# A dense piece between the halves of the scores, loads spread out, and reciprocals as exp(-ln(sum)) in a fused top-k attention and feed-forward kernel

## The chip, the cores and the metric

The kernel runs on one core of one Trainium2 chip. The metric is the device time of one execution in microseconds; lower is better. The kernel before has a median of 922.19 us over three runs (918.74, 922.19 and 922.97).

Five engines work side by side, each through its own list of instructions in order: TensorE (PE, matrix products; PEld is its loading of weights), VectorE (DVE), ScalarE (ACT), GpSimd (POOL) and SyncE (SP, which here only issues transfers). They wait for each other through semaphores. ScalarE and GpSimd issue transfers from their own lists too.

## The reference, cut to what matters

```python
batch, n_heads, seq, head_dim = (8, 8, 576, 64)
...
scores = scale * np.matmul(q, k.transpose(0, 1, 3, 2))
kth = np.partition(scores, -top_k, axis=-1)[..., -top_k:-top_k + 1]     # top_k = 32
mask = scores >= kth
scores = np.where(mask, scores, -1000000000.0)
scores = scores - np.max(scores, axis=-1, keepdims=True)
attn = np.exp(scores)
attn = attn / (np.sum(attn, axis=-1, keepdims=True) + 1e-09)
out = np.matmul(attn, v)                       # top-k attention, 64 heads
...
x = out.transpose(0, 2, 1, 3).reshape(4608, 512)
h = np.maximum(x @ w_in, 0.0)                  # w_in 512 x 2048
y = h * h @ w_out                              # w_out 2048 x 512
```

For every row of scores the 32 largest of 576 are kept, their softmax weighs the values, and each token's 512 numbers then go through a two-layer network whose middle is squared after the ReLU.

## The kernel before, in words

**Steps.** Everything is driven by a loop over U = 144 steps (`for u in range(U)`, near the end of the listing). A step is two tiles of 128 rows of scores, 576 columns each; nine tiles make a pair of heads, and there are 32 pairs. All engines' lists are written out by hand: `pin` keeps the order in which the code emits the instructions. Work on one tile is spread over several passes of the loop, so in pass u the code emits parts of steps u - 4 to u + 1:

- `drop(u-1)`: ScalarE negates the row maximum and the 32nd value (`neg`, L384); GpSimd marks what lies under the 32nd value (`gone`, L399). The marks are added to the scores `s`, by GpSimd itself in the first 11 steps (`EARLY`, L401), and by a transfer that accumulates later on (L403).
- `quads_of(u)` and `topk(u)`, VectorE: the columns are first folded into maxima and minima of pairs and quads, then four rounds of MAX8 and MATCH_REPLACE8 (L365, L369) find the 32 largest. `quads_of` (L315, L316) reads the tile `most`.
- `invert(u-4)`, VectorE: the reciprocal of the row sums (`rsum`, L465). The sums come with the products of weights and values in a PSUM tile, `av_ps`.
- `scores(u+1)`: TensorE computes the scores in two halves of 288 columns into the PSUM banks `sc_a` and `sc_b` (L284), and ScalarE copies both into `s` (L289). `sc_a` is free again once VectorE's L307 has read it, `sc_b` once L316 has (L306 leaves an interim result there). GpSimd then adds the halves (`both`, L330).
- `prepare`: part of the preparation of a coming pair of heads, with transposes on TensorE through the two PSUM buffers named `gen`, and copies on ScalarE (qkT, qbd, and casts of values).
- `place(u-4)`, ScalarE: the finished rows, scaled by `rsum`, go into `x_tok` (L481) or `x_rem` (L486).
- `exps(u-2)`, ScalarE (L407), then `turn(u-2)`: a transposing transfer from SyncE's list (`wT`, L416). `fetch` issues loads of later pairs on the same list: up to 10 a step while u < 8, 3 afterwards.
- `pairs_of(u+1)`, VectorE (L306, L307, and L309 in the first steps); `copy_far`, ScalarE (the second half of `most`, L322); `lesser`, GpSimd (L339).
- two calls of `dense`, then `products(u-3)`: TensorE weighs the values with `wT` (L451).
- `load_weights(1)`: one load of w_in or w_out from GpSimd's list (L694), 12 in all, three of them ahead of the loop.

**The feed-forward network** is cut into pieces that fill TensorE's gaps. When all 512 numbers of a chunk of 128 tokens are there, `turn_x` puts the chunk's turning into `moves`: four transposes on TensorE into a `gen` buffer (L520) and a copy by ScalarE (`xT`, L526). Afterwards the chunk's block can start: an up piece is 16 matmuls into a `gen` buffer (L569), and on ScalarE a ReLU (`rl`, L574) and a square (`h`, L580); a down piece is 4 matmuls into `dn_ps` (L612), and after the fourth of them ScalarE copies the result (`wide`, L620) and SyncE stores it. `dense` emits at most one turning and one or two pieces; `piece` alternates between ups and downs; with no piece there, `idle_piece` runs four matmuls on constants (L633). A block may start one step after its chunk was turned (`ripe`), in the last 12 steps (`Z`) at the second `dense` of the same step (`fresh`). There, the turning stands right before and between the exponentials instead.

**Behind the loop** the last two steps are turned by TensorE, and what is left of ups and downs is worked off.

The functions that the change touches, and what calls them:

## Time and profile before

| | |
|---|---|
| runs of the kernel before | 922.19, 922.97, 918.74 us |
| the profiled execution | 920.99 us |
| its span, first to last instruction | 919.1 us |
| VectorE busy | 882.8 us, 96% |
| ScalarE busy | 762.3 us, 83% |
| GpSimd busy | 776.8 us, 85% |
| TensorE busy (matmul, weight loads) | 687.5 us, 441.3 us |
| granted TensorE clock, mean | 0.927 |

Times in the profile are us from the span's start unless marked ns. A line of the timeline gives start, duration, engine, source line, operation, what is written and read, and how many were merged; a bracket gives the idle time ahead of it and what ended it. Durations of neighbours on one engine overlap, since an instruction is only done when its last results are written; the distance from one start to the next is what an instruction costs its engine. A line of the waits reads "engine, line waited for: us in total, times, longest". SPq, ACTq and POOLq are the issuing of transfers from those lists.

### The profile page before, as it was taken

The page shows a single profiled execution, that of the slowest core. Times are in us where ns is not written, and L with a number is a line of the kernel's source. Part 1 is how long each engine was busy: PE and PEld are TensorE (multiplying, and loading weights), DVE is VectorE, ACT ScalarE, POOL GpSimd, SP SyncE. Part 2 cuts the span into 40 slices and gives each one's busy share as a digit, 9 for nine tenths or more (in the row PEclk, how much of TensorE's full clock was granted, in tenths as well). Part 3 has the DMA queues.
Part 4 walks back from the last instruction along what each step waited for, and adds up shares of the span by engine and source line. Part 5 has one row for each costly group of instructions (what it writes and reads, how often), then busy time and mean ns, then how long its engine had stood idle before and what let it go on. Part 6 is the DMA issues. An engine that isn't in the chain of part 4 may idle for free.

```text
span 919.1 us, 21088 instructions
## 1 busy us (share of the span) xinstructions
PE 687.5 (75%) x6268; PEld 441.3 (48%) x6268; DVE 882.8 (96%) x3632; ACT 762.3 (83%) x1755; POOL 776.8 (85%) x804
## 2 busy tenths in 40 slices
PE   6766777777677777777776877777787777878777
PEld 3333354445454444444454545454554444555545
DVE  6997999999999999999999999999999999898995
ACT  4655689888988998988988898988988988897884
POOL 7987988888988889888899888988789898787880
PEclk9998989998999999999999799999979998999899
DMA  8597798999997999889898999989899999676762
GB/s 166 78 146 136 155 179 199 195 183 219 181 197 174 203 197 201 197 180 201 195 198 192 197 191 192 203 189 200 177 187 203 198 206 203 141 163 152 167 129 52
DMA packets 290489, 163.60 MB, mean 178 GB/s; under 512 B 258112, under 2 KB 268608, under 8 KB 290368
## 3 DMA queue, kind: packets, MB, share of 16 engines
q1 hardware_dynamic: 267408, 80.29, 46.5%
q0 software_dynamic: 21616, 81.47, 39.9%
q8 instruction: 52, 0.85, 0.4%
q14 instruction: 69, 0.57, 0.2%
q10 hardware_dynamic: 1344, 0.43, 0.2%
HBM read 37.75 MB, written 9.44 MB: 51 GB/s over the span
## 4 chain that ended last, share of the span: by engine, by line
DVE 67%; issue 12%; PE 9%; ACT 7%; DMA 5%; POOL 0%; SPq 0%; ACTq 0%; POOLq 0%; DVEq 0%
DVE m L365 27%; DVE cat L369 18%; DVE sc_b L306 6%; DVE cat L316 5%; DVE cat L315 5%; DVE most L307 5%; DMA s<-gone_b 2%; PE sc_b L284 2%; PE gen L569 2%; PE sc_a L284 1%; DMA wT<-w_two_a 1%; PE dn_ps L612 1%; ACT s L289 1%; DVE rsum L465 1%; ACT x_tok L481 1%
## 5 line engine op out<-in xcount | busy, mean ns | idle before, releaser
L365 DVE MAX8 m<-cat 128x8 f32<-128x104 f32 (+3 forms) x1152 | 438.4, 422 | 0.0
L369 DVE MATCH_REPLACE8 cat<-m,cat 128x104 f32<-128x104 f32 (+2 forms) x864 | 262.9, 311 | 0.0
L330 POOL TENSOR_TENSOR cat<-s 128x576 int32<-128x576 int32 (+1 forms) x144 | 237.9, 1652 | 4.6 <-ACT s L289 4.6
L339 POOL TENSOR_TENSOR cat<-cat,most 128x576 int32<-128x576 int32 (+1 forms) x144 | 195.6, 1359 | 19.3 <-ACT most L322 5.4
L284 PE MATMUL sc_b<-qkT 64*128 64x288 f32 x512 | 106.8, 492 | 116.5 <-DVE cat L316 111.9
L569 PEld LDWEIGHTS <-w_in 128*128 128x128 bf16 x2304 | 155.2, 105 | 46.3 <-issue 25.4
L612 PE MATMUL dn_ps<-w_out,h 128*128 128x512 bf16 x560 | 161.8, 421 | 0.0
L569 PE MATMUL gen<-xT,w_in 128*128 128x128 bf16 x2000 | 144.9, 231 | 7.7 <-ACT xT L526 4.8
L289 ACT ACTIVATE s<-sc_b 128x576 f32<-128x576 f32 x144 | 93.3, 648 | 60.2 <-PE sc_b L284 53.7
L399 POOL TENSOR_SCALAR gone_b<-s,neg 128x576 uint8<-128x576 f32 x142 | 105.9, 746 | 30.9 <-ACT neg L384 21.3
L284 PEld LDWEIGHTS sc_b<-qkT 64*128 64x128 f32 x512 | 46.0, 202 | 167.6 <-issue 87.8
L284 PE MATMUL sc_a<-qkT 64*128 64x288 f32 x512 | 101.0, 470 | 28.3 <-DVE most L307 26.2
L399 POOL TENSOR_SCALAR gone_a<-s,neg 128x576 uint8<-128x576 f32 x143 | 106.6, 745 | 18.1 <-ACT neg L384 7.2
L289 ACT ACTIVATE s<-sc_a 128x576 f32<-128x576 f32 x144 | 91.3, 634 | 23.7 <-PE sc_a L284 21.8
L451 PEld LDWEIGHTS <-wT 128*128 128x128 bf16 (+1 forms) x1600 | 60.1, 103 | 63.9 <-DMA wT<-w_two_c 24.6
L574 ACT ACTIVATE rl<-gen 128x512 f32<-128x512 f32 x141 | 84.3, 598 | 7.1 <-PE gen L569 6.7
L580 ACT ACTIVATE h<-rl 128x512 bf16<-128x512 f32 x136 | 85.7, 630 | 4.3
L612 PEld LDWEIGHTS <-h 128*128 128x128 bf16 x560 | 53.5, 105 | 58.9 <-issue 25.5
L403 POOL DMA_DIRECT2D s<-gone_b x66 | 58.4, 884 | 21.7 <-DVE cat L369 8.1
L403 POOL DMA_DIRECT2D s<-gone_a x65 | 57.4, 883 | 20.2 <-DVE cat L369 10.6
L407 ACT ACTIVATE w_two_a<-s,neg 128x576 bf16<-128x576 f32 x96 | 69.7, 781 | 3.9 <-DMA s<-gone_b 3.4
L407 ACT ACTIVATE w_two_c<-s,neg 128x576 bf16<-128x576 f32 x94 | 68.1, 781 | 3.3 <-DMA s<-gone_b 2.7
(170 smaller groups left out, 1194.8 us busy)
## 6 DMA issues: line engine op xcount, KB each, us to landing
s<-gone_b POOLq DMA_DIRECT2D x66, 576.0 KB, 4.7
s<-gone_a POOLq DMA_DIRECT2D x65, 576.0 KB, 4.7
v_raw<-in_v_dram SPq DMA_DIRECT2D x64, 128.0 KB, 3.2
k_raw<-in_k_dram SPq DMA_DIRECT2D x63, 128.0 KB, 3.6
q_raw<-in_q_dram SPq DMA_DIRECT2D x63, 128.0 KB, 3.2
out_dram<-wide SPq DMA_DIRECT2D x31, 256.0 KB, 3.2
v_raw<-in_v_dram SPq DMA_DIRECT2D x64, 32.0 KB, 3.2
w_in<-in_moe_w_in_dram POOLq DMA_DIRECT2D x8, 256.0 KB, 5.5
```

What stands on the lines that cost most here:

```text
L284: pin(nc.tensor.matmul(out=ps[j][:, x, 0:HALF], lhsT=lhsT, rhs=rhs, start=True, stop=True))
L289: pin(nc.scalar.activation(s[:, :, j * HALF:(j + 1) * HALF], ps[j][:, :, 0:HALF], AF.Copy))
L330: pin(tt(less, s[:, :, 0:wide].bitcast(i32), s[:, :, HALF:HALF + wide].bitcast(i32), op=ALU.add))
L339: pin(tt(less, less, d["most"][:, 0:n_h, :, :].bitcast(i32).rearrange("p h x n -> p x h n"), op=ALU.subtract))
L365: pin(nc.vector.max(out=m[r][:, x, :], in_=part(r, x)))
L369: pin(nc.vector.match_replace(out=part(r, x), in_to_replace=m[r][:, x, :], in_values=part(r, x), imm_value=NEG))
L399: pin(nc.gpsimd.tensor_scalar(byte[:, x, :, 1], s[:, x, :], scalar1=d["neg"][:, x, 1:2], scalar2=-HUGE, op0=ALU.add, op1=ALU.mult))
L403: pin(nc.gpsimd.dma_start(out=s[:, :, :].rearrange("p x n -> p (x n)"), in_=byte[:, :, :, :].rearrange("p x n two -> p (x n two)").bitcast ...
L407: pin(nc.scalar.activation(w_two[u % 3][:, x, 0:S], d["s"][:, x, :], AF.Exp, bias=d["neg"][:, x, 0:1]))
L569: pin(nc.tensor.matmul(out=hp[:, n * n_rows:(n + 1) * n_rows], lhsT=w_in[:, kh, (f0 + n) * 128:(f0 + n + 1) * 128], rhs=xt(kh), start=(kh ...
L580: pin(nc.scalar.activation(h2, flat, AF.Square))
L612: pin(nc.tensor.matmul(out=op[:, :], lhsT=held["h2"][:, f, c * 128:(c + 1) * 128], rhs=w_out[:, f, :], start=(f == 0), stop=(f == NF - 1)))
```

## The change

Line numbers in the profiles of the kernel before are those of the old file. The change does six things.

1. **Reciprocals.** For all steps but the last 12, `invert` is a logarithm of the two sums on ScalarE, and `place` begins with exp(-ln) on ScalarE, which gives `rsum`. A table set that holds both functions is loaded as ScalarE's first instruction; it was loaded ahead of the first copy (L199), behind three load issues.
2. **A dense piece between the halves.** `scores(u+1)` emits the first half, its copy, then `dense(u, 0)` (a turning if there is one, and a piece), and only then the second half and its copy. The second `dense` stays where both were. The order of pieces is fixed: ups first between the halves, downs first in the second call.
3. **A chunk's turning** is queued right after `place` in every step and is emitted between the halves in the next pass; the special places in the last 12 steps go. The block starts at the second `dense` of the pass that turned it.
4. **Loads spread.** `fetch` takes 4 loads a step while u < 12 instead of 10 while u < 8; w_out is loaded in 8 parts instead of 4, so `load_weights` goes on for four more steps.
5. **In the last 20 steps** a step has three pieces: two stood in the first call of `dense` and one in the second; now it is one and two (three in step U - 2).
6. A down block that ended in the second call keeps the next one from starting in the same step.

```diff
+    nc.scalar.preload_act_table_set("natural_log_exp_and_others")
...
-    def scores(u):
+    def scores(u, between=None):
...
+        half(js[0])
+        if not between:
+            half(js[1])
...
             pin(nc.scalar.activation(s[:, :, j * HALF:(j + 1) * HALF], ps[j][:, :, 0:HALF], AF.Copy))
             if u == 0 and j == 1:
                 pairs_of(0)
+            if between and j == js[0]:
+                between()
+                half(js[1])
...
     def invert(u):
-        r = small.tile([128, 2, 1], f32, name="rsum", bufs=4)
-        pin(nc.vector.reciprocal(r[:, :, :], sums(u)[:, :, 64:65]))
-        st[u]["r"] = r
+        r = st[u]["r"] = small.tile([128, 2, 1], f32, name="rsum", bufs=4)
+        if u >= U - 12:
+            pin(nc.vector.reciprocal(r[:, :, :], sums(u)[:, :, 64:65]))
+            return
+        ln = st[u]["ln"] = small.tile([128, 2, 1], f32, name="lnsum", bufs=4)
+        pin(nc.scalar.activation(ln[:, :, :], sums(u)[:, :, 64:65], AF.Ln))
...
     def place(u):
+        if "ln" in st[u]:
+            pin(nc.scalar.activation(st[u]["r"][:, :, :], st[u]["ln"][:, :, :], AF.Exp, scale=-1.0))
...
-                elif at_step[0] >= Z:
+                else:
                     fresh.append(done)
-                else:
-                    ripe.setdefault(at_step[0] + 1, []).append(done)
...
-    def piece(later=False, most=10 ** 6):
+    def piece(later=False, most=10 ** 6, first=None):
         turn_of[0] ^= 1
-        for q_ in ((ups, downs), (downs, ups))[turn_of[0]]:
+        for q_ in ((ups, downs), (downs, ups))[turn_of[0] if first is None else first]:
...
-                if q_ is downs and q_[0].part == 3:
+                if q_ is downs and q_[0].part == 3 and first is not None and phase[0]:
                     shut[0] = at_step[0]
...
     def dense(u, x, later=False):
-        for go in ripe.pop(u, ()):
-            go()
+        phase[0] = x
         if x == 0:
+            ups_now[0] = 0
             if moves:
                 moves.pop(0)()()
-            ups_now[0] = 0
         else:
-            moves.extend(soon_moves)
-            soon_moves.clear()
             while fresh:
                 fresh.pop(0)()
-        N = 2 if u >= U - 20 and x == 0 else 1
-        for n in range(N):
-            if not piece(later, most_ups(u)) and n == 0:
+        for n in range(1 if u < U - 20 or x == 0 else 3 if u == U - 2 else 2):
+            if not piece(later, most_ups(u), (x + n) % 2) and n == 0 and shut[0] != u:
                 idle_piece()
...
-    for g in range(4):
-        rows = moe_w_out.rearrange("(f p) n -> p f n", p=128)[:, 4 * g:4 * g + 4, :]
-        w_loads.append((w_out[:, 4 * g:4 * g + 4, :], rows))
+    for g in range(8):
+        rows = moe_w_out.rearrange("(f p) n -> p f n", p=128)[:, 2 * g:2 * g + 2, :]
+        w_loads.append((w_out[:, 2 * g:2 * g + 2, :], rows))
...
-            scores(u + 1)
+            scores(u + 1, (lambda: dense(u, 0)) if u else None)
...
-        copies = []
-        if u >= Z:
-            turn_x(u)
-            moves.extend(soon_moves)
-            soon_moves.clear()
-            copies = [go() for go in moves]
-            moves.clear()
+        turn_x(u)
+        moves.extend(soon_moves)
+        soon_moves.clear()
         if u == U - 1:
-            copies.pop(0)()
+            moves.pop(0)()()
         if ok(u - 2):
             exps(u - 2, 0)
-            while copies:
-                copies.pop(0)()
             exps(u - 2, 1)
             turn(u - 2)
-        fetch(10 if u < 8 else 3)
+        fetch(4 if u < 12 else 3)
...
         if u < U - 1:
-            dense(u, 0)
+            if u == 0:
+                dense(u, 0)
             dense(u, 1)
...
         products(u - 3)
-        turn_x(u)
         load_weights(1)
```

More of the change, by code (lines that the diff above doesn't have):

```diff
@@ L269, with half @@
     st = {}
-    def scores(u):
+    def scores(u, between=None):
         ps = [ps_sc.tile([128, 2, 512], f32, name=f"sc_{j}") for j in "ab"]
         js = (1, 0) if u < 2 else (0, 1)
-        for j in js:
+        def half(j):
             for x, (i, c, a) in enumerate(steps[u]):
@@ L494 @@
     soon_moves = []
-    ripe = {}
     late, tail = [], []
@@ L636 @@
     behind, fresh = [], []
-    shut = [-1]
+    shut, phase = [-1], [0]
     ups_now = [0]
-    def piece(later=False, most=10 ** 6):
+    def piece(later=False, most=10 ** 6, first=None):
         turn_of[0] ^= 1
-        for q_ in ((ups, downs), (downs, ups))[turn_of[0]]:
+        for q_ in ((ups, downs), (downs, ups))[turn_of[0] if first is None else first]:
             if q_ is ups and ups_now[0] >= most:
@@ L733 @@
     soon.pop(0)()
-    Z = U - 12
     at_step = [0]
@@ L811 @@
             early_exps(u, 1)
-            piece(True)
-            piece(True)
+            piece(True, first=1)
+            piece(True, first=0)
         products(u - 3)
-        turn_x(u)
         load_weights(1)
@@ L825, in flush @@
             behind.pop(0)()
-    assert not ripe and not moves and not soon_moves
+    assert not fresh and not moves and not soon_moves
     late.append(True)
@@ L867 @@
             pin(nc.scalar.activation(bad[:, :], count[0:1, 0:1], AF.Copy))
-    assert not ripe and not moves and not soon_moves
+    assert not fresh and not moves and not soon_moves
     fast.close()
```

## The prediction, made before the changed kernel ran

> **What bounds the kernel now.** I read the page's busy shares first, then its chain that ended last, then VectorE's waits by stretch of time.
>
> ```profile
> span 919.1 us, 21088 instructions
> PE 687.5 (75%) x6268; PEld 441.3 (48%) x6268; DVE 882.8 (96%) x3632; ACT 762.3 (83%) x1755; POOL 776.8 (85%) x804
> DVE 67%; issue 12%; PE 9%; ACT 7%; DMA 5%; POOL 0%; SPq 0%; ACTq 0%; POOLq 0%; DVEq 0%
> ```
>
> VectorE is busy 96% of the span and holds 67% of the chain; everyone else has air. Its idle time sits in few places. The answers below are its waits in 50 to 92 us (steps 7 to 11), 92 to 780 and 780 to 880; each row gives who waited for whom, the us in total, the times and the longest.
>
> ```profile
> DVE rsum L465 <- PE av_ps L451: 4.8, 3, 2.7
> DVE sc_b L306 <- ACT s L289: 1.0, 3, 0.3
> DVE cat L315 <- ACT most L322: 0.9, 1, 0.9
> ...
> DVE cat L315 <- ACT most L322: 1.6, 4, 0.9
> DVE rsum L465 <- PE av_ps L451: 1.0, 1, 1.0
> ...
> DVE rsum L465 <- PE av_ps L451: 5.3, 3, 2.6
> DVE sc_b L306 <- ACT s L289: 1.1, 1, 1.1
> DVE cat L315 <- ACT most L322: 0.4, 1, 0.4
> ```
>
> So 6.7 us are lost early, 2.6 us in the 688 us of the middle, 6.8 us late. One step of the middle on VectorE:
>
> ```profile
> 510.73 0.16 DVE L465 RECIPROCAL rsum<-av_ps 128x2 f32<-128x2 f32 x1
> 510.81 0.45 DVE L365 MAX8 m<-cat 128x8 f32<-128x120 f32 x2
> 513.14 0.45 DVE L306 TENSOR_TENSOR sc_b<-sc_a,s 128x288 f32<-128x288 f32 x1
> 513.87 1.41 DVE L365 MAX8 m<-cat 128x8 f32<-128x576 f32 x2
> 519.14 0.45 DVE L306 TENSOR_TENSOR sc_b<-sc_a,s 128x288 f32<-128x288 f32 x1
> 521.20 0.43 DVE L315 TENSOR_TENSOR cat<-sc_b,most 128x288 f32<-128x288 f32 x1
> ```
>
> A step is 519.14 - 513.14 = 6.00 us, VectorE's own work without a gap. What the others do in a step counts only once it no longer fits.
>
> **Reciprocals (L465): -10.6 us.** A reciprocal lasts 0.16 us, but its successor starts after 510.81 - 510.73 = 0.08 us: consecutive instructions overlap. 132 of 144 go to ScalarE, so 132 x 0.08 = 10.6 us, and a step becomes 5.92 us. Taking 0.16 each would promise 21 us, which the overlap denies. The 4.8 + 1.0 + 5.3 = 11.1 us that the reciprocals waited do not go by themselves: on TensorE the late products (L451) stand ahead of the next scores, so VectorE would wait at L306 instead. For the same reason the new wait on ScalarE, Ln for those products, costs nothing of its own, though the s copies, the squares and the exponentials are queued behind it: the first s copy needs scores that TensorE issues after the products.
>
> **Loads spread (SyncE's queue, steps 0 to 11): -3.2 us of the early 6.7.** SyncE's queue, ScalarE and TensorE around the first early wait:
>
> ```profile
> 43.83 1.34 SPq L110 DMA_DIRECT2D q_raw<-in_q_dram  x2
> 49.84 1.28 SPq L117 DMA_DIRECT2D v_raw<-in_v_dram  x2
> 51.23 2.00 SPq L416 DMA_TRANSPOSE wT<-w_two_a  x1
> ...
> 46.02 1.44 ACT L407 ACTIVATE w_two_a<-s,neg 128x576 bf16<-128x576 f32 x2
> ...
> 57.34 0.54 PEld L451 LDWEIGHTS <-wT 128*128 128x128 bf16 x10 [5.53 <-DMA wT<-w_two_a]
> ```
>
> The weights were ready at 46.02 + 1.44 = 47.46, but ten loads held the queue from 43.83 to 51.12, so the transpose went out 3.8 us late and TensorE waited 5.5 us for it. In the changed order 4 loads (6 once) stand between two transposes, 2.9 us at this rate; that wait goes. What is late next is GpSimd, whose queue also issues the weight loads:
>
> ```profile
> 36.99 0.74 POOL L399 TENSOR_SCALAR gone_b<-s,neg 128x576 uint8<-128x576 f32 x1
> 42.88 0.56 POOL L694 DMA_DIRECT2D w_in<-in_moe_w_in_dram  x1
> 43.52 0.74 POOL L399 TENSOR_SCALAR gone_a<-s,neg 128x576 uint8<-128x576 f32 x1
> ...
> 89.01 0.75 POOL L399 TENSOR_SCALAR gone_a<-s,neg 128x576 uint8<-128x576 f32 x1
> 96.25 1.57 POOL L399 TENSOR_SCALAR gone_b<-s,neg 128x576 uint8<-128x576 f32 x2
> ...
> 93.55 0.21 ACT L384 ACTIVATE neg<-m 128x4 f32<-128x4 f32 x1 [1.15 <-DVE m L365]
> ```
>
> Its round with a weight load is 43.52 - 36.99 = 6.53 us, of which the load takes 43.52 - 42.88 = 0.64. The round that ends at 96.25 has no load and takes 7.24 us, since it still does the last early masking and already the wide sums; at its end GpSimd is 96.25 - 93.55 = 2.7 us behind the value it needs, and VectorE does not feel that. After the change the loads go on to step 12 (8 halves of w_out, as large as a w_in load, in place of 4), and VectorE no longer pauses so that GpSimd can catch up. Estimate: rounds 2 to 9 lose 0.3 us each against VectorE's early step, rounds 10 and 11 lose 7.24 + 0.64 - 6.0 = 1.9 each: 8 x 0.3 + 2 x 1.9 = 6.2 us behind, where 2.7 was harmless. So 3.5 of the 6.7 us come back as waits for GpSimd's results. Bounds: nothing gained, and all 6.7.
>
> **Table load first (L49 of the changed kernel): +1.3 us.**
>
> ```profile
> 0.76 0.67 ACTq L142 DMA_DIRECT2D k_raw<-in_k_dram  x1
> 2.82 1.28 ACT L199 ACT_TABLE_LOAD   x1 [2.82 <-issue]
> 4.14 1.09 PE L188 MATMUL gen<-id_f,k_raw 128*128 128x128 f32 x4 [4.14 <-DMA k_raw<-in_k_dram]
> ```
>
> Now it lies behind ScalarE's three load issues, hidden by the flight of the loads; then it stands ahead of them, and TensorE's first work waits for k. Its 1.28 us are the most that it can cost; nothing, if an issue can pass a running table load. I take 1.3, as the row shows the two one after the other.
>
> **A dense piece between the halves, and ln/exp on ScalarE: +4 us in the middle.** TensorE and ScalarE in the middle:
>
> ```profile
> 512.19 1.06 PE L569 MATMUL gen<-xT,w_in 128*128 128x128 bf16 x16
> 516.15 0.76 PE L284 MATMUL sc_b<-qkT 64*128 64x288 f32 x4 [1.29 <-DVE cat L316]
> ...
> 516.17 0.19 ACT L384 ACTIVATE neg<-m 128x4 f32<-128x4 f32 x1
> 516.27 0.63 ACT L289 ACTIVATE s<-sc_a 128x576 f32<-128x576 f32 x1
> 519.83 0.41 ACT L322 ACTIVATE most<-sc_b 128x288 f32<-128x288 f32 x1
> 520.12 0.61 ACT L574 ACTIVATE rl<-gen 128x512 f32<-128x512 f32 x1
> 520.76 0.63 ACT L580 ACTIVATE h<-rl 128x512 bf16<-128x512 f32 x1
> 521.31 0.21 ACT L384 ACTIVATE neg<-m 128x4 f32<-128x4 f32 x1
> ...
> 120.00:780.00 660.00, 495.43 (x4663) 323.11 (x4662) 657.39 (x2736) 586.53 (x1357) 578.10 (x567) 0.92 0.94 194
> ```
>
> TensorE stands idle 1.29 us before the second half, because that bank is free only after L316; an up piece lasts 1.06 us, so it fits there for nothing. ScalarE pays. The last row (busy PE, PEld, DVE, ACT, POOL of 120 to 780 us, PEclk, DMA share, GB/s) gives it 586.53 of 660 us, 5.33 us a step. The trace has no Ln; the nearest row is neg, as small: 0.10 us to the next start (516.27 - 516.17). The Exp feeds the x_tok copies right behind it, so its whole 0.2 us count and a gap, as rl before h takes 0.64 for 0.61. Together 0.33 us (bounds 0.2, both by starts, and 0.45, both whole), so 5.66 of 5.92 us: 96% full. That fits, but order matters too. L315 waits for the most copy; here that ended at 520.24, 0.96 us ahead of L315 at 521.20. After the change rl, h (0.64 + 0.55), Ln and Exp stand ahead of it: 1.5 us more. Against that, neg may start sooner: its MAX8 ended at 513.87 + 1.41 = 515.28, and it ran at 516.17 because rl and h came first; 0.9 us back. Net 0.6 us later: some 0.35 us of slack are left, and none in a step that also copies one of the 32 turned chunks (rl's size). I charge such a step 0.1 us, and a little for stretches of slow clock: 4 us in all. Bounds: 0, and 36 (0.3 us in 120 steps, if neg gains nothing).
>
> A rule bears on the clock; PEclk is 0.92 in that row. The Trainium skill (TensorE: Matmul & The Clock Gate, "Part 1: The HAM clock gate (the "warmup" mystery)") says that TensorE's clock is halved after a window of about 3.4 us with too little activity. By it, a piece moved into the gap would raise PEclk, and the 4 us would be nearer 2.
>
> **Late stage: -1.5 us.** The copy of a turned chunk now follows the first s copy, so the next piece gets its PSUM buffer sooner; but steps 124 to 130 hold two pieces and ln/exp. Of 6.8 us I take 1.5 back (bounds: 6 back, 3 more lost). What is left to do behind the last step is the same work.
>
> **Sum** on the profiled execution's 920.99 us (1.89 beside its span): -10.6 - 3.2 + 1.3 + 4 - 1.5 = -10.0, so 911. That execution stands 1.2 us under the runs' median of 922.19 and within their spread, so I shift nothing.
>
> **Rivals.**
> - ScalarE is full: its addition is nearer 0.45 us, and each middle step loses 0.08 us more: 120 x 0.08 = 9.6, about 921. For it: 96% full. Against: L315's waits in the middle are only 1.6 us now.
> - Slower: most is late in every step, because neg gains nothing from the new order (output copies, value casts and late scores keep ScalarE busy until then). At 0.3 us a step the middle loses 36 instead of 4: 943. It decides against the change from 0.15 us a step (the gain of 10.0, the 4 charged, and 4.6 for half a per cent, over 120 steps). Against: the 0.9 us above.
> - Better: GpSimd's backlog is harmless, the middle has no new stalls, the table load is hidden, 5 of the late waits go: 920.99 - 10.6 - 6.7 - 5 = 899.
> - Not what it says: each Ln and each Exp loads a table, 264 x 1.28 = 338 us, about 1250. Against: in the changed program's order ScalarE has one table load, and Copy, Relu and Exp share one in this trace. The Trainium skill (ScalarE: Activation LUTs, "Table sets: the hidden batching unit") names a set with both exp and ln, which speaks against it too.
>
> **How the numbers follow.** Forecast 911 (902 to 918): 0.50. Better, 899: 0.17. ScalarE full, 921: 0.18. Slower, 943: 0.14. Tables: 0.01. The range 899 to 922 leaves out the slower cases and a little on either side. A measurement of this kernel can tell about 0.5% from no change: under 917.6 is faster (0.66, a little of the forecast's case being above), over 926.8 slower (0.15), the rest 0.19.
>
> **What would show it.** Right: VectorE steps of 5.92 us in the middle; L315 waiting for most there 3 to 6 us; no wait for wT before 80 us, but waits at 80 to 105 us that end at GpSimd or at s; TensorE's first matmul near 5.4 us; ScalarE 95% busy. L315's waits over 18 us are the slower rival. Steps still at 6.00 would make the first term wrong, early waits of under 1 us the second.

## The result, and the profile after

The changed kernel took 929.64 us (median of 6 runs) beside 922.36 us for the kernel before in the same job: ratio **1.0119, 95% interval 1.0082 to 1.0157**. The ratio is formed from fast executions alone (one of the six, 944.18 us, was slow), so it isn't the quotient of the two medians, 1.008. Forecast were 911 us and a faster kernel; it became slower. In the profile of after, the old L306, L315, L322, L451, L465 and L481 are L315, L324, L331, L460, L475 and L495.

From the page of after, span, busy shares and the chain that ended last, by engine and by line:

```profile
span 927.1 us, 21006 instructions
PE 678.1 (73%) x6186; PEld 422.6 (46%) x6264; DVE 878.4 (95%) x3500; ACT 792.7 (86%) x2019; POOL 780.0 (84%) x808
...
DVE 34%; ACT 22%; DMA 13%; PE 9%; issue 8%; SPq 1%; POOL 1%; ACTq 0%; POOLq 0%; DVEq 0%
DVE m L374 13%; DVE cat L378 9%; ACT s L295 4%; DMA wT<-w_two_b 4%; DMA wT<-w_two_a 4%; PE gen L580 3%; DMA wT<-w_two_c 3%; DVE sc_b L315 3%; ACT rl L585 3%; ACT h L591 3%; DVE cat L324 3%; DVE most L316 3%; DVE cat L325 2%; ACT w_two_c L416 2%; PE sc_a L286 2%
```

VectorE's busy share fell by a point only, but its share of the chain was halved, from 67% to 34%. In its place stand ScalarE (22% for 7%) and transfers (13% for 5%), all of these named being transfers of wT. A chain that was one engine's has become a chain through four. That is the first thing to look at when a kernel whose bound engine was relieved gets no faster.

Where the time went: the three stretches up to step 20, steps 20 to 120, and the rest, cut at the starts of VectorE's first instruction of a step (columns: length; busy time of PE, PEld, DVE, ACT, POOL; PEclk, DMA share, GB/s). Before, then after:

```profile
9.22:140.76 131.54, 94.69 (x646) 53.73 (x646) 123.36 (x505) 85.15 (x202) 112.62 (x123) 0.92 0.81 145
140.76:742.51 601.75, 450.23 (x4226) 291.67 (x4227) 600.32 (x2501) 535.00 (x1238) 527.99 (x516) 0.93 0.94 194
742.51:919.10 176.59, 138.37 (x1384) 93.36 (x1382) 158.42 (x626) 139.58 (x314) 128.24 (x126) 0.93 0.70 149
```

```profile
9.20:136.84 127.64, 92.32 (x637) 48.12 (x646) 122.03 (x490) 88.92 (x234) 115.08 (x126) 0.95 0.82 149
136.84:755.01 618.17, 449.35 (x4185) 286.09 (x4239) 597.93 (x2402) 558.09 (x1438) 528.21 (x517) 0.95 0.91 190
755.01:927.10 172.09, 132.09 (x1350) 85.85 (x1365) 157.75 (x610) 143.09 (x346) 128.79 (x126) 0.97 0.73 152
```

The first stretch gave 131.54 - 127.64 = 3.9 us, the last 4.5, and the hundred steps between took 618.17 - 601.75 = 16.4 us: together +8.0, which is 927.1 - 919.1. The middle is the whole question. VectorE's waits there (112 to 780 us), and ahead of them those of 80 to 112 us:

```profile
DVE cat L324 <- ACT most L331: 2.5, 2, 1.9
DVE m L374 <- POOL cat L348: 2.0, 2, 1.5
...
DVE sc_b L315 <- ACT s L295: 9.8, 9, 3.6
DVE cat L324 <- ACT most L331: 9.5, 20, 0.9
```

All of the middle's waits end at ScalarE. One place shows how. Four steps of after, one window each, and three of before:

```profile
526.88:532.82 5.94, 4.45 (x58) 2.67 (x58) 5.94 (x26) 5.33 (x14) 5.34 (x7) 1.00 0.98 224
532.82:538.75 5.93, 5.00 (x37) 3.50 (x35) 5.93 (x26) 4.81 (x12) 5.38 (x7) 0.71 0.74 161
538.75:545.41 6.66, 5.24 (x47) 3.02 (x46) 6.03 (x26) 6.56 (x19) 4.69 (x5) 1.00 0.76 170
545.41:551.47 6.06, 3.80 (x39) 2.54 (x40) 6.04 (x25) 5.92 (x18) 5.24 (x6) 1.00 0.95 223
```

```profile
519.14:525.14 6.00, 4.09 (x23) 1.72 (x22) 6.00 (x26) 4.51 (x12) 5.45 (x7) 0.71 1.13 228
525.14:531.14 6.00, 6.00 (x63) 4.67 (x62) 6.00 (x26) 5.11 (x13) 4.97 (x6) 0.72 0.79 178
531.14:537.14 6.00, 4.81 (x58) 3.38 (x54) 6.00 (x26) 5.97 (x15) 5.10 (x7) 1.00 1.06 172
```

The first two rows show the step that was forecast: 5.93 to 5.94 us for 6.00 before. In the second, PEclk is 0.71, because TensorE's clock was halved for 3.41 us. ScalarE fell behind in it: its exponentials began 0.75 us ahead of this step (532.07) and 1.00 us behind the start of the next (539.75). The next step held 6.56 us of work for it, VectorE waited, and the step took 6.66. Before, two steps in a row at 0.71 and 0.72 cost nothing. The trace's records of the granted clock have 22 such stretches in steps 20 to 120 of before (88.7 us, and 1.8 us lost over 100 x 6.00), and 17 in after (61.4 us, and 25.2 lost over 100 x 5.93). Of after's loss 20 us lie in the 34 steps in or just behind a stretch. So it isn't the clock that got worse; the slack that absorbed such stretches is gone. That the stretches cause the loss isn't shown by this: a step that stalls also gives TensorE less to do.

What has no slack is a circle that takes two steps. In steps 20 to 120 the chain that ended last passes through a transfer of wT fifteen times in after (91 us), and never in before. One such turn, from the timeline of after (rows of TensorE, ScalarE and SyncE's queue that make the circle; a bracket is the idle time and what ended it):

```profile
575.87 1.43 ACT L416 ACTIVATE w_two_b<-s,neg 128x576 bf16<-128x576 f32 x2
577.33 2.32 SPq L425 DMA_TRANSPOSE wT<-w_two_b  x1
...
584.12 0.48 PE L460 MATMUL av_ps<-vau_a,wT 128*128 128x65 bf16 x10 [3.25 <-DMA wT<-w_two_b]
584.53 0.76 PE L286 MATMUL sc_a<-qkT 64*128 64x288 f32 x4
585.22 1.07 PE L580 MATMUL gen<-xT,w_in 128*128 128x128 bf16 x16
...
586.33 0.60 ACT L585 ACTIVATE rl<-gen 128x512 f32<-128x512 f32 x1 [0.26 <-PE gen L580]
586.96 0.63 ACT L591 ACTIVATE h<-rl 128x512 bf16<-128x512 f32 x1
587.49 0.63 ACT L295 ACTIVATE s<-sc_b 128x576 f32<-128x576 f32 x1
588.02 0.59 ACT L176 ACTIVATE qkT<-gen 128x512 f32<-128x512 f32 x1
588.50 0.20 ACT L487 ACTIVATE rsum<-lnsum 128x2 f32<-128x2 f32 x1
588.73 0.52 ACT L495 ACTIVATE x_tok<-av_ps,rsum 128x64 bf16<-128x64 f32 x2
589.14 1.44 ACT L416 ACTIVATE w_two_a<-s,neg 128x576 bf16<-128x576 f32 x2
```

The exponentials (575.87) are turned by a transfer (577.33), for which the products wait until 584.12; behind them in TensorE's list stand the first scores and the piece between; behind that piece, in ScalarE's list, rl, h, the second copy of s, a copy that prepares a coming pair (qkT), Exp, x_tok, and the exponentials of two steps later (589.14). That is 589.14 - 575.87 = 13.27 us where two steps are 11.86. Behind them the copy of most came late, and VectorE waited 0.60 us for it at 590.91.

Half clock can't be the only trigger, since the granted clock was 1.00 throughout this turn. Fourteen of the fifteen turns lie wholly in these steps, from 12.0 to 16.8 us long; in six of them the clock was full, and these took 12.0 to 13.3. Long transfers may be another: the fourteen took 4.9 to 7.4 us from issue to landing (6.75 here), where the medians of all transfers, by the three buffers that they read, are 4.1 to 4.6. In before these medians are 4.9 to 5.2, and little was lost: there, rl and h belonged to pieces behind the top-k work and ran behind the copy of most, so the second copy of s waited for no piece of its own step.

### The profile page after: what moved, and what is told of

It is laid out like the page before. It is cut to its first block, busy times and chain, and to the rows that moved or that the text cites. A ratio compares the mean times of both kernels' runs of the same rounds, so it can differ in the third digit from the quotient of the medians.

```text
span 927.1 us, 21006 instructions
## 1 busy us (share of the span) xinstructions
PE 678.1 (73%) x6186; PEld 422.6 (46%) x6264; DVE 878.4 (95%) x3500; ACT 792.7 (86%) x2019; POOL 780.0 (84%) x808
## 4 chain that ended last, share of the span: by engine, by line
DVE 34%; ACT 22%; DMA 13%; PE 9%; issue 8%; SPq 1%; POOL 1%; ACTq 0%; POOLq 0%; DVEq 0%
DVE m L374 13%; DVE cat L378 9%; ACT s L295 4%; DMA wT<-w_two_b 4%; DMA wT<-w_two_a 4%; PE gen L580 3%; DMA wT<-w_two_c 3%; DVE sc_b L315 3%; ACT rl L585 3%; ACT h L591 3%; DVE cat L324 3%; DVE most L316 3%; DVE cat L325 2%; ACT w_two_c L416 2%; PE sc_a L286 2%
## 5 line engine op out<-in xcount | busy, mean ns | idle before, releaser
L374 DVE MAX8 m<-cat 128x8 f32<-128x104 f32 (+3 forms) x1152 | 439.7, 423 | 2.0 <-POOL cat L348 2.0
L339 POOL TENSOR_TENSOR cat<-s 128x576 int32<-128x576 int32 (+1 forms) x144 | 235.1, 1633 | 10.6 <-ACT s L295 8.1
L348 POOL TENSOR_TENSOR cat<-cat,most 128x576 int32<-128x576 int32 (+1 forms) x144 | 195.9, 1361 | 41.6 <-ACT most L331 32.0
L580 PEld LDWEIGHTS <-w_in 128*128 128x128 bf16 x2304 | 145.2, 103 | 41.8 <-issue 37.5
L460 PEld LDWEIGHTS <-wT 128*128 128x128 bf16 (+1 forms) x1600 | 60.0, 100 | 211.6 <-issue 56.4
L623 PE MATMUL dn_ps<-w_out,h 128*128 128x512 bf16 x490 | 131.3, 384 | 7.8 <-issue 4.4
L408 POOL TENSOR_SCALAR gone_a<-s,neg 128x576 uint8<-128x576 f32 x143 | 106.6, 745 | 14.3 <-ACT neg L393 1.7
L315 DVE TENSOR_TENSOR sc_b<-sc_a,s 128x288 f32<-128x288 f32 x144 | 65.7, 456 | 14.8 <-ACT s L295 12.1
L324 DVE TENSOR_TENSOR cat<-sc_b,most 128x288 f32<-128x288 f32 x144 | 63.9, 444 | 15.5 <-ACT most L331 13.9
L623 PEld LDWEIGHTS <-h 128*128 128x128 bf16 x560 | 50.0, 99 | 58.0 <-issue 19.6
L412 POOL DMA_DIRECT2D s<-gone_a x65 | 57.4, 884 | 20.2 <-DVE m L374 12.8
```

The source lines that it names most:

```text
L339: pin(tt(less, s[:, :, 0:wide].bitcast(i32), s[:, :, HALF:HALF + wide].bitcast(i32), op=ALU.add))
L348: pin(tt(less, less, d["most"][:, 0:n_h, :, :].bitcast(i32).rearrange("p h x n -> p x h n"), op=ALU.subtract))
L374: pin(nc.vector.max(out=m[r][:, x, :], in_=part(r, x)))
L408: pin(nc.gpsimd.tensor_scalar(byte[:, x, :, 1], s[:, x, :], scalar1=d["neg"][:, x, 1:2], scalar2=-HUGE, op0=ALU.add, op1=ALU.mult))
L412: pin(nc.gpsimd.dma_start(out=s[:, :, :].rearrange("p x n -> p (x n)"), in_=byte[:, :, :, :].rearrange("p x n two -> p (x n two)").bitcast ...
L580: pin(nc.tensor.matmul(out=hp[:, n * n_rows:(n + 1) * n_rows], lhsT=w_in[:, kh, (f0 + n) * 128:(f0 + n + 1) * 128], rhs=xt(kh), start=(kh ...
```

## The experiments

Three theories stood at the start. **LOOP**: the circle just shown. **RING**: a shorter one of one step, through the products' single bank `av_ps` (x_tok, products, sc_a, piece between, rl, h, s, Exp, x_tok). **FULL**: ScalarE has too little slack, whatever the order. Ratios are to the kernel before, in the same job; "lost" is the length of steps 20 to 120 less 100 unstalled steps (593 us with logarithms, 600 with VectorE's reciprocals), in one profiled execution. It is good to some 7 us: before, e7 and e8 have the same steps there and lost 1.8, 1.9 and 8.6 (4.9 of the last in one wait), and e1 and e13, alike there too, 3.4 and 6.8.

### First job: parts of the change

**e1, no piece between the halves** (the turning too goes back to the step's end):

```diff
-            scores(u + 1, (lambda: dense(u, 0)) if u else None)
+            scores(u + 1)
...
-            if u == 0:
-                dense(u, 0)
+            dense(u, 0)
             dense(u, 1)
...
         products(u - 3)
+        if u < U - 2:
+            turn_x(u)
```

> The changed kernel (929.6 us; VectorE's steps 20 to 120 take 618.2 us there, 601.8 before) with both dense calls back behind the top-k, all else kept: ln/exp on ScalarE, loads spread. Theory RING: the dense piece between the halves closes a ring that has to go round once a step: x_tok copies (ScalarE) free the only bank of av_ps, products (TensorE), first half of the scores, up piece, rl and h (ScalarE), second copy of s, Exp, x_tok. Without the piece the ring is some 2 us shorter: steps 20 to 120 in 593 to 598 us, total 904 to 910 us. Theory FULL: ScalarE simply has too much to do since ln and exp came to it; the place of the piece does not matter: steps 20 to 120 stay near 618, total near 927 to 930.

926.27 us, 1.0065 [1.0033, 1.0097]; the profiled execution is its fastest (919.82). There the middle was 596.4 us, 3.4 lost, but steps 120 to 143 took 148.9 us for 141.9 in after. The piece between costs the middle and pays late; neither theory had the late loss.

**e2, all reciprocals on VectorE**, the rest as in after:

```diff
-        if u >= U - 12:
+        if True:
```

> The changed kernel with all reciprocals on VectorE again, the piece still between the halves. FULL: ScalarE is relieved by 0.33 us a step, so the waits go and VectorE's step is 6.00: steps 20 to 120 in 601 to 604 us, total 911 to 915 us. RING: the ring is only 0.3 us shorter against a step that is 0.08 us longer, so many of the waits stay: steps 20 to 120 in 608 to 615, total 918 to 926.

919.98 us, 0.9989 [0.9954, 1.0024]. Its profiled execution was its slowest (928.0 us, 14.9 lost), so here the runs decide: without the logarithms the kernel is as fast as before. That lies in RING's range (918 to 926), not in FULL's (911 to 915).

**e3, the piece's ScalarE part late** (rl, h and wide of the piece between behind the copy of most; the matmuls stay):

```diff
-            scores(u + 1, (lambda: dense(u, 0)) if u else None)
+            scores(u + 1, (lambda: dense(u, 0, True)) if u else None)
...
+            while behind:
+                behind.pop(0)()
```

> The changed kernel; TensorE's part of the piece stays between the halves, but ScalarE's part of it (rl and h, or wide) is emitted behind the most copy as in the kernel before. ScalarE's work is the same in sum. RING: rl and h are out of the ring (1.2 us, and the wait for the up piece), steps 20 to 120 in 593 to 600 us, total 904 to 911. FULL: nothing changes, 927 to 930.

943.15 us, 1.0255 [1.0193, 1.0317]. The middle was as long as in after (618.2 us, 25.2 lost), and its 12 us more came behind step 120 (939.2 - 756.0 = 183.2 us for 172.1). Neither theory had expected that. The trace shows why the middle gained nothing: the second copy of s still stands behind the piece, since TensorE does the second half of the scores after it. Waits of ScalarE for that half in 112 to 780 us of after, then of this kernel:

```profile
ACT s L295 <- PE sc_b L286: 2.6, 6, 0.8
```

```profile
ACT s L295 <- PE sc_b L286: 39.8, 44, 2.3
```

In after the second copy of s began 0.28 us (median) behind the end of those scores, here 0.05. So taking rl and h out shortened the circle by 0.2 to 0.3 us only, not by their 1.2, and the chain passes through transfers of wT sixteen times, as often as in after. Why the end of the kernel was slower stays unexplained.

**e4, logarithms alone**, put into the kernel before with the early table load (items as in the change):

```diff
+        ln = st[u]["ln"] = small.tile([128, 2, 1], f32, name="lnsum", bufs=4)
+        pin(nc.scalar.activation(ln[:, :, :], sums(u)[:, :, 64:65], AF.Ln))
```

> The kernel before with ln/exp on ScalarE and the table load first, nothing else of the change. RING: the step becomes 5.93 and the waits stay away, steps 20 to 120 in 594 to 598 us; the early waits stay, moved from the reciprocal to L306; total 909 to 914 us. FULL: ScalarE's waits come here as well, steps 20 to 120 in 610 to 618, total 922 to 930.

922.98 us, 1.0008 [0.9975, 1.0041], with unstalled steps of 5.93 us that should have been worth 1.1%. In its profile, of its slowest execution (926.11 us), 11.7 were lost in the middle, and VectorE waited 10.4 us for ScalarE (112 to 780 us). The saving of VectorE isn't seen in the runs, even with no piece between.

### Second job: the circles, and the loads

**e5, x_tok first**: Exp and the x_tok copies ahead of the copies of the scores.

```diff
+            if ok(u - 4):
+                place(u - 4)
             scores(u + 1, (lambda: dense(u, 0)) if u else None)
```

> The kernel after, with one step moved: the Exp of the sums' logarithms and the copies of the weighted values into x_tok are put into ScalarE's order ahead of the copies of the scores of the next step, instead of behind both of them and the chunk work between. Theory RING (products, av bank, x_tok and the piece between the halves hang on each other once per step): x_tok no longer waits for sc_a, the up piece, rl, h and s_b, the wait of TensorE's first product (L460) for x_tok goes from 64 us to under 10, and steps 20 to 120 fall from 618 us to 593 to 600; total 904 to 914. Theory LOOP (the exponentials, the wT transfer, the products and the chunk work between take two steps together, and nothing is over): the loop still holds s_b ahead of the exponentials, so the middle stays at 612 to 620 and the total at 925 to 932. Theory FULL (ScalarE has too little slack): the same work, 925 to 932.

933.97 us, 1.0119 [1.0042, 1.0196], 24.1 lost. The wait for x_tok vanished from TensorE's list of waits, the waits for wT stayed (122 us, of TensorE's weight loads in 112 to 780 us), and so did the loss. RING falls.

**e6, products a step later**, up to the 112th step, with a fourth buffer of wT and a seventh of the values:

```diff
+        w = u - 5 if u <= C + 1 else u - 4
...
-        products(u - 3)
+        if u <= C:
+            products(u - 4)
```

> The kernel after, with products, sums and placing of x one step later in all steps up to the 112th (one more buffer of wT and one more of the values), so that a block has three steps instead of two from its exponentials to its products. Nothing else is moved and no work is added. Theory LOOP (two steps through the wT transfer are full): TensorE's and its weight load's waits for wT (83 us and 152 us after) go to under 20 each, steps 20 to 112 run at 5.93 to 5.98 each, and the total is 904 to 912. Theory RING (the av bank's one step): its order is unchanged, so the middle stays at 612 to 620 and the total at 925 to 932. Theory FULL: 925 to 932.

919.47 us, 0.9976 [0.9940, 1.0013]; the middle fell from 618.2 to 607.3. Waits for wT and x_tok in 112 to 780 us of after, then of this kernel:

```profile
PE av_ps L460 <- ACT x_tok L495: 55.3, 57, 1.6
PEld L460 <- DMA wT<-w_two_a: 48.6, 32, 3.0
PEld L460 <- DMA wT<-w_two_b: 48.3, 30, 4.2
...
PEld L460 <- DMA wT<-w_two_c: 38.8, 31, 4.0
```

```profile
PE av_ps L460 <- ACT x_tok L495: 88.1, 95, 2.7
...
PEld L460 <- DMA wT<-w_two_a: 3.5, 3, 1.8
PEld L460 <- DMA wT<-w_two_c: 3.3, 3, 1.7
PEld L460 <- DMA wT<-w_two_b: 2.4, 3, 1.0
```

135.7 us of the weight loads' waiting for wT became 9.2, the chain passes through a transfer of wT once instead of fifteen times, and the ratio fell by 1.4%. TensorE's longer wait for x_tok did no harm that e10 could find. LOOP is right in kind, and too large in size: it expected 904 to 912.

**e7, loads spread** alone in the kernel before, and **e8**, the same with w_out still in four loads:

```diff
-        fetch(10 if u < 8 else 3)
+        fetch(4 if u < 12 else 3)
```

> The kernel before, with the loads alone spread as in the kernel after (four a step for 12 steps instead of ten for 8; w_out in eight loads of half the size). No theory of the middle touches it: steps 20 to 120 as before, 600 to 603. Steps 0 to 12 fall by 7 to 8 us against before, steps 12 to 16 rise by 4 to 5 where GpSimd catches up (as in the kernel after), and the total is 915 to 919 if these two do not depend on the piece between; if they do, 920 to 925.

> The kernel before, with the loads spread over 12 steps but w_out still in four loads. If the stall in steps 12 to 16 is GpSimd catching up on the work that the faster first steps bring sooner, it stays (28 to 29 us for four steps, against 24 before) and the total is as with the loads spread and w_out halved. If the smaller w_out loads make it, the stall goes and the total is 3 to 5 us lower, 911 to 915.

923.21 us, 1.0022 [0.9985, 1.0059], and 920.24 us, 0.9976 [0.9941, 1.0011]. In their profiles steps 0 to 20 took 128.2 and 129.2 us for 131.5 before; the runs as a whole show no gain that can be told from none. Steps 12 to 20 took 53.2 and 52.9 us for 49.4: the stall there doesn't come from the halved loads.

### Third job: is it the step, and what is left?

**e9**, a fourth buffer of wT and nothing else; then products later with x_tok first (**e10**), with no piece between (**e11**), and with reciprocals by VectorE (**e12**); the edits are those above, put together.

```diff
-name="wT", bufs=3)
+name="wT", bufs=4)
```

> The kernel after with four buffers of wT instead of three, and nothing else. Putting the products a step later brought the ratio from 1.012 to 0.998, and that kernel had four such buffers too. If it was the buffer (the transposing DMA waiting for the products to free one), this one falls as far: 917 to 922, middle (steps 20 to 120) 605 to 610. If it was the third step between exponentials and products (theory LOOP), this one stays at 926 to 933, middle 614 to 620, with wT waits on TensorE of 60 to 90 us.

> The kernel after with the products a step later (steps up to the 112th) and the copies of x_tok ahead of the copies of the scores: both changes that were made singly before. The later products alone left a middle of 607 us over an ideal 593, with 88 us of TensorE's products waiting for x_tok. If the rest is that one-step loop (RING now behind LOOP), the wait goes under 10 us, the middle comes to 593 to 599 and the total to 905 to 914. If ScalarE's lack of slack makes the rest (FULL), the middle stays at 604 to 612 and the total at 915 to 925.

> The kernel after with the products a step later and both chunk pieces behind the top-k work as in the kernel before (no piece between the halves); the reciprocals by ScalarE and the spread loads stay. With the piece behind alone the ratio was 1.0065, with a middle of 597. LOOP and RING both leave nothing here: middle 593 to 596, and the total is what the late steps leave, 910 to 920. If FULL still costs something, the middle is 597 to 605 and the total 918 to 926.

> The kernel after with the products a step later and all reciprocals by VectorE. An unstalled step is then 6.00 us, a middle of 600, instead of 5.93. If ScalarE's 0.25 us a step of Ln and Exp makes what is left over in the later-products kernel (607 against 593), this one's middle is 600 to 603, with waits of VectorE under 3 us, and the total 915 to 922: the gain of the reciprocals is given back in full. If something else makes the rest, it shows here too: middle 607 to 614, total 923 to 930.

The buffer: 929.03 us, 1.0108 [1.0071, 1.0146]. It was the step, not the buffer of wT (the seventh of the values wasn't tried alone). With x_tok first: 922.72 us, 1.0015 [0.9996, 1.0035], 11.4 lost; RING isn't behind LOOP either. With no piece between: 936.41 us, 1.0179 [1.0136, 1.0221], 12.8 lost, and steps 120 to 143 took 153.6 us. That was a miss on both accounts and stays unexplained; its granted clock, 0.909, was among the lowest. With VectorE's reciprocals: 919.64 us, 0.9983 [0.9956, 1.0011], 5.0 lost, as FULL expected. It equals the same kernel with logarithms (0.9976): as far as the runs can tell, ScalarE's share gives the gain back in full.

Steps 20 to 120 of the kernel with logarithms alone, of products later, and of products later with VectorE's reciprocals:

```profile
141.50:746.18 604.68, 446.70 (x4177) 292.67 (x4227) 595.87 (x2401) 557.63 (x1439) 528.01 (x516) 0.92 0.92 193
```

```profile
138.60:745.94 607.34, 441.19 (x4195) 282.29 (x4248) 596.19 (x2401) 558.67 (x1443) 529.36 (x517) 0.97 0.93 193
```

```profile
138.42:743.40 604.98, 440.04 (x4205) 281.11 (x4257) 601.38 (x2503) 534.68 (x1240) 529.82 (x517) 0.97 0.92 194
```

ScalarE (the fourth busy time) has 558 us to do in the first two, 94% of 593 unstalled us, and 535 in the third, 89% of 600. The kernels with 558 lose 11.7 and 14.3 us there, the one with 535 loses 5.0. These are single executions: e8, with 535, lost 8.6, and e1 and e13, with 556 and 557, 3.4 and 6.8. So FULL rests on the ratios of the runs; that the busy time sets the loss isn't shown.

### Fourth and fifth job: the clock, and a better order

**e13, piece between from step 124 on only** (the turning at the step's end up to there), and **e16**, the same with VectorE's reciprocals:

```diff
-            scores(u + 1, (lambda: dense(u, 0)) if u else None)
+            scores(u + 1, (lambda: dense(u, 0)) if u >= U - 20 else None)
```

> The kernel after with the piece and the chunk's turning between the halves of the scores only from step 124 on; up to there both pieces stand behind the top-k work and the turning at the step's end. Theory: the piece between costs in the middle alone, where every step is close to full, and pays in the last twenty steps. Steps 20 to 120 then run as with no piece between (597), steps 124 to 143 and the tail as in the kernel after (118 and 30), and the total is 908 to 916, below both kernels. Rival: the late steps owe their gain to blocks that the piece between finished earlier, and then 124 to 143 stays at 122 to 126 and the total at 918 to 926.

> The kernel of e13 with all reciprocals by VectorE, so that of the change only the spread loads and the order of the last twenty steps are left. If the logarithms gain in the middle what they seem to (7 us less what they lose by waits, some 4 us net where no piece stands between), this one is 3 to 6 us slower than e13: 912 to 920. If ScalarE's extra work loses as much as VectorE gains, it is equal to e13 or faster, 908 to 914.

918.62 us, **0.9960 [0.9938, 0.9982]**, and 920.40 us, 0.9984 [0.9961, 1.0007]. The first is the only kernel whose interval lies under the kernel before. It is 0.4%, not the 1% hoped for, and the two aren't told apart. Its steps 124 to 143 took 120.8 us, between the 118 of the theory and the 122 of its rival. Steps 20 to 120 of the first:

```profile
139.84:739.64 599.80, 452.85 (x4238) 296.65 (x4238) 595.08 (x2401) 556.98 (x1439) 529.01 (x517) 0.92 0.95 195
```

6.8 us are lost, less than half of the loss with the logarithms and the piece between.

**e14, half of each down piece, and e15, half of each up piece**: in the steps up to 124 every second matmul with w_out, or with w_in, is left out.

```diff
-                for f in range(4 * part, 4 * part + 4):
+                fs = range(4 * part, 4 * part + 4)[::2 if at_step[0] < U - 20 else 1]
+                for f in fs:
```

> The kernel after, leaving out half of the products with w_out in the steps up to 124 (two matmuls of 512 columns instead of four per down piece, so its output is not the reference's). The piece between the halves is an up piece in most steps and keeps its whole length; TensorE has some 0.45 us a step less to do behind the top-k work. Theory CLOCK (the loop is just full, and stretches at half clock are what it cannot take): fewer such stretches, under 8 of them in steps 20 to 120 instead of 17, and the middle falls to 596 to 606. Theory LENGTH (the piece between is too long at any clock): the middle stays at 612 to 620.

> The kernel after, leaving out half of the products with w_in in the steps up to 124 (eight matmuls of 128 columns instead of sixteen per up piece, so its output is not the reference's). The piece between lasts about half as long. Theories CLOCK and LENGTH both expect the middle at 594 to 602; if it stays above 608, neither TensorE's length nor its clock is in the loop, and ScalarE's order alone (rl and h ahead of the copies of the scores) is.

Their middles, half down pieces first:

```profile
138.96:768.66 629.70, 449.68 (x4038) 290.72 (x4039) 600.91 (x2401) 560.37 (x1438) 529.12 (x517) 0.87 0.88 186
```

```profile
138.46:753.45 614.99, 441.86 (x3438) 250.51 (x3439) 597.30 (x2402) 559.66 (x1435) 527.80 (x517) 0.88 0.92 191
```

Both expectations were turned round: 940.13 us, 1.0165 [1.0122, 1.0208], and 928.38 us, 1.0066 [1.0039, 1.0093]. TensorE had less to do, its granted clock fell from 0.95 to 0.87 and 0.88, and half-clock time rose from 61 us to 160 and 143. The middle lost 36.7 and 22.0 us. A lighter TensorE got a lower clock. What a stretch costs can't be read from these runs: with half down and half up pieces, 74 and 73 of the hundred steps lie in or behind a stretch, and hold nearly all of the loss (35 and 22 us), but in before 65 do, and hold 1.8.

**e17 and e18, filler**: two matmuls of 382 columns into an unread part of the bank `av_ps`, in after ahead of the products, and in the kernel of e13 between the halves.

```diff
+            pin(nc.tensor.matmul(out=avb[:, 130:512], lhsT=id_h[:, :], rhs=fill[:, 0:382], start=True, stop=True))
```

> The kernel after with two matmuls of 382 columns ahead of the products in the steps up to 124, into a part of the products' bank that nobody reads: TensorE has some 0.4 us a step more to do, at the place where it waits 1.4 us a step for wT and x_tok. Theory CLOCK (half-clock stretches, which come when TensorE has too little to do, are what the full loop cannot take): under 8 half-clock stretches in steps 20 to 120 instead of 17, granted clock 0.98 or more, the middle 600 to 610, total 912 to 922. Rival (the clock goes along, it does not cause): the clock may rise, but the middle stays at 614 to 622, total 926 to 934.

> The kernel of e13 (piece between only from step 124) with the same two filler matmuls between the halves of the scores up to step 124, where TensorE waits 0.7 us a step for sc_b to come free. Theory CLOCK: the half-clock time of steps 20 to 120 falls from 96 us to under 50, the middle from 599.8 to 594 to 597, total 911 to 917. Rival: there is slack enough without a piece between, so that the clock is worth nothing, and the filler's 0.4 us delays sc_b in part of the steps: middle 599 to 606, total 918 to 925.

933.58 us, 1.0138 [1.0107, 1.0168], and 988.45 us, 1.0738 [1.0706, 1.0769]. The second was no test: the filler had to wait for the logarithm that reads the same tile, as TensorE's first wait shows (L646 is the filler there).

```profile
PE av_ps L646 <- ACT lnsum L481: 130.8, 77, 3.1
```

The first raised the granted clock to 0.98 and halved the half-clock time (27 us), and still lost 21.6 us, as the rival expected; but its filler too waited for x_tok (92.5 us), so its 0.4 us lie inside the circle. What the clock alone is worth stays open.

## Why the prediction was wrong, point by point

- **Reciprocals, -10.6.** The size of the unstalled step was right: 5.93 to 5.94 us for a forecast 5.92. That this reaches the end was wrong. Three pairs that differ in the logarithms alone (the first in the early table load too) show it: before and e4 (1.0008), e12 and e6 (0.9983 and 0.9976), e16 and e13 (0.9984 and 0.9960). Of the forecast 1.1%, between -0.1 and 0.24% is left, and each ratio is uncertain by 0.2 to 0.4% either way; and in after itself the logarithms cost 1.3% (e2).
- **Loads spread, -3.2.** Right in the profile, in mechanism and nearly in size: step 20 was reached 3.9 us sooner, after 74.7 us for steps 0 to 12 (82.2 before) and 52.9 for 12 to 20 (49.4). Some 1.1 of that are reciprocals (16 x 0.07); the five profiles with spread loads and VectorE's reciprocals (e2, e7, e8, e12, e16) gained 1.6 to 3.3 there. The waits that came back stand where they were expected, at 92 to 109 us, and begin at GpSimd: 2.0 us straight (`L374 <- POOL cat L348`), and the longest, 1.9 us for most, behind exponentials that waited 2.6 us for the transfer of GpSimd's marks (`s<-gone_a`). In the runs of the loads alone it can't be seen.
- **Table load, +1.3.** Wrong, it cost no more than 0.1. The rows below show ScalarE loading its table and issuing a transfer at the same time; TensorE began at 4.23 us for 4.14 before.

```profile
0.76 1.28 ACT L49 ACT_TABLE_LOAD   x1 [0.76 <-PEq L982]
0.79 0.66 ACTq L143 DMA_DIRECT2D k_raw<-in_k_dram  x1
...
4.23 1.09 PE L189 MATMUL gen<-id_f,k_raw 128*128 128x128 f32 x4 [4.23 <-DMA k_raw<-in_k_dram]
```

- **Piece between and logarithms on ScalarE, +4. This is the step that failed**: it measured 25.2 - 1.8 = 23 us. Two sentences of it are wrong. "An up piece lasts 1.06 us, so it fits there for nothing" counted TensorE's gap, the engines' loads and, for ScalarE, how late the copy of most would be. It didn't follow the piece, rl and h further: ahead of the second copy of s, and through it of the exponentials and the transfer for the products two steps on. That circle was never added up; giving it one more step (e6) took back 11 us of the middle and 1.4% of the time. And "a little for stretches of slow clock" took the slack of before for granted, in which 22 such stretches stood beside a loss of 1.8 us. ScalarE's addition itself was sized somewhat too high: 0.28 us a step by the distances to the next start (medians of 0.05 behind Ln and 0.23 behind Exp), 0.23 by busy time (535.00 / 100 to 558.09 / 100), for a forecast 0.33.
- **The rule on the clock.** PEclk of the middle rose from 0.93 to 0.95, and it fell to 0.87 when down pieces were halved. Both agree with the Trainium skill (TensorE: Matmul & The Clock Gate, "Part 1: The HAM clock gate (the "warmup" mystery)"), by which too little activity halves the clock. That the 4 us would thus be nearer 2 was wrong: the clock rose and the middle lost 23 us more.
- **Late stage, -1.5.** 4.5 us were gained behind step 120 (172.1 us for 176.6), inside its bounds, so the term was too small by 3. The logarithms have no visible part in it: e2 and e12, without them, took 171.6 and 171.8 us there. This is the part of the change that pays, but e13, which keeps only the order of the last twenty steps, took 175.0 us and so holds 1.6 of the 4.5.
- **The rivals.** "ScalarE is full" (921) and "most late in every step" (943) lie on both sides of 929.64. The waits for most came to 9.5 us in 20 places, far from every step; as much again (9.8) was lost earlier in the step, at L315, because the copy of s was late. No rival named the circle.

What the runs show: the loss needs the circle through wT and the logarithms both, since giving the circle a step (e6) or taking the logarithms out (e2) brings the time back to that of before, and doing both (e12) brings no more. The chain agrees: it passes a transfer of wT fifteen and sixteen times in the middles of after and e3, once in those of e6, e1, e10 and e11; between them stand e2's slowest execution (ten) and e4's (six). What stays open: why e3 and e11 lost as much late as they did; why e11's middle, without the circle in its chain, lost 12.8 us; and how much of the loss is triggered by half clock and how much by long transfers.

## What to carry to other kernels

Before moving work between engines, add up the circles, not only the loads: follow each result through every engine's list until it comes back to its own buffer or list, in us, and compare that with the steps it may take. A gap of one engine isn't free if something behind the filler, in another engine's list, feeds the next turn of such a circle. And a saving on the bound engine is worth what the next engine has to spare: with ScalarE at 94% of the step, VectorE's 0.07 us a step brought no gain clear of noise in any of three pairs of kernels.

## What the runs showed of the hardware

- TensorE's granted clock fell when its work was reduced: 0.95, 0.88 and 0.87 with whole pieces, half up and half down pieces, and 0.98 with filler added ahead of the products (e17). Of the 589 half-clock stretches in the twenty traces, 571 last 3.41 us or a multiple of it.
- A table load of 1.28 us ran on ScalarE beside the issuing of transfers from its own list.
- Ln and Exp of 128 x 2 values last 0.15 and 0.20 us and added 0.23 us a step to ScalarE's busy time; the reciprocal of the same values, 0.16 us long, was worth 0.07 us a step on VectorE.
